# Attention into a sine-activated MLP on one core: alpha's load, the opening's casts and batch 1's transposes, x and v casts rearranged

## The chip, the cores and the metric

The kernel runs on one core of a Trainium2 chip, in one launch. The metric is the device time of an execution in microseconds (us). TensorE (PE) multiplies and transposes, VectorE (DVE), ScalarE (ACT) and GpSimd (POOL) do the rest, SyncE (SP) issues most of the DMAs, POOL some of them and ACT two.

## What is computed

```python
# q, k, v: (8 batches, 8 heads, 576 rows, 64); x: (4608, 512)
q_s = softmax(q, axis=-1)              # over the 64 entries of a head's row
k_s = softmax(k, axis=2)               # over the 576 rows
kv = einsum('bhsd,bhse->bhde', k_s, v) # a 64x64 matrix for each head
x = einsum('bhsd,bhde->bhse', q_s, kv) # transposed to (B*S, H*D) = (4608, 512)
h = x @ w_in                           # w_in (512, 2048)
g = h + sin(alpha * h)**2 / alpha      # alpha: 2048 values
out = g @ w_out                        # w_out (2048, 512), out (4608, 512)
```

The inputs are float32, the matmuls run in bf16.

## The kernel before, in words

The 4608 tokens are worked in nine stages t of 512 tokens. In a stage `mm_h` makes 16 tiles h (ni = 0 to 15), each by four 128x512 matmuls over the four column groups of x; ScalarE takes the sine (`sine`, L269), one of ScalarE, POOL and VectorE squares it (L271, L273, L275), VectorE combines it with h into g (`combine`, L279), and `mm_o` (L283) multiplies g by w_out, 64 matmuls to a stage. x comes from the attention of one batch at a time: exp of q and k on ScalarE (L119), v cast to bf16 with a column of ones, `kv_mm` (L174, 36 small matmuls for each half of the heads), `kv_norm` (L184, L185) which divides by the sums and gives `kbd`, q normalized (`qn`) and transposed (`tp`, L201, copied to `qT`), and `attn_x` (L218), whose result is copied to `xT`.

The order of the work on each engine is the order in which the program writes it. Nothing reorders it, so an instruction that waits holds up all that stand behind it on its engine. A DMA queue issues in that order too. PSUM banks come from pools of one or two buffers each ("a", "b", "l", "k"): a tile waits until the one before it in its buffer has been read.

**The opening** (L308 to L407) does batch 0. SyncE loads q, k and v in halves ("half" means the head pairs `ii` = 0 and 1), POOL the second half of v in two pieces (L308 from L341 and L342), then w_in in column pieces and w_out (L109, L112). ScalarE's queue loads alpha (L313), and TensorE transposes it ahead of everything else (L329); VectorE copies it and takes its reciprocal (L330, L331). The first x is copied to `xT` by VectorE and ScalarE (L393, L394), the second by VectorE twice (L405); ScalarE copies the second half of the transposed queries (L395) and casts the last four row blocks of v's second half, then loads the Sin table (L396). Of the tiles h, the parts that need only the first x run before the second x.

**Stage 0's tiles** (L407 to L460) carry the loads of batch 1 in `late`: after tile 6 the first half of q, after tile 8 and 10 pieces of w_out, after tile 13 the second half of q, and k and v in halves. A 1-element copy on VectorE into the tile (L443) makes the q loads wait for that place in VectorE's order, and SyncE's order makes the others wait behind them.

**Batch 1's attention** stands inside the 64 output matmuls of stage 0 (`o_quad`; `take(os, n)` puts the next n of them into TensorE's order). Here `norm_q` (L153) has POOL multiply the first half of q and VectorE the second; `cast_v1` (L474) casts one half of v on ScalarE and one on VectorE, all nine row blocks at a time; `transpose_q1` (L482) transposes one half and copies it on VectorE; `x_half` (L491) computes one half of x. After the first `kv_norm`, SyncE loads the leftover rows of q of batches 0 and 1 (`q8`, L497, again behind 1-element copies on VectorE, L496), and batch 2. After the second x, ScalarE takes exp of q8 and loads the Sin table again for stage 1 (L509). In stage 1, after tile 11, q8 is transposed (L523).

Of the kernel before, what the change touches and what calls it, by code (L numbers as in the profile page):

```python
# [15 lines left out]
F32 = mybir.dt.float32  # L16
BF16 = mybir.dt.bfloat16
# [6 lines left out]
def kernel(  # L24
# [78 lines left out]
        load("k", k, b)  # L103
        load("v", v, b)

    def load_win(c0, c1, k0=0, k1=4):
        n, kk = slice(c0, c1), slice(k0, k1)
        for x in range(2):
            nc.gpsimd.dma_start(out=win[64 * x:64 * x + 64, kk, n], in_=win_v[x][:, kk, n])  # L109

    def load_wout(n0, n1):
        nc.gpsimd.dma_start(out=wout[:, n0:n1, :], in_=wout_v[:, n0:n1, :])  # L112
# [66 lines left out]
    def kv_norm(b, i0=0, i1=2):  # L179

        kt, m = kbd[b % 2], i1 - i0
        kvr = small.tile([128, 2, 2], F32, name="kvr")[:, :, 0:m]
        src = A["kvp", b][:, :, i0 * 65:i1 * 65].rearrange("p e (ii c) -> p e ii c", ii=m)
        nc.vector.reciprocal(kvr, src[:, :, :, D])  # L184
        nc.vector.tensor_tensor(kt[:, :, i0:i1], src[:, :, :, 0:D],  # L185
                                kvr.unsqueeze(3).to_broadcast([128, 2, m, D]), op=ALU.mult)

    def q_tile(b):
        if ("qT", b) not in A:
            A["qT", b] = att2.tile([128, 2, J, 128], BF16, name="qT")  # L190
        return A["qT", b]
# [6 lines left out]
    def q_transpose_ii(b, ii, j0, j1, tp):  # L198

        for j in range(j0, j1):  # L200
            nc.tensor.transpose(tp[:, j - j0], A["qn", b][:, ii, j], identb)  # L201
# [108 lines left out]

    for n, t, ii in (("q", q, 0), ("k", k, 0), ("q", q, 1), ("v", v, 0), ("k", k, 1)):
        load0(nc.sync, n, t, ii, 0, 8 if n == "q" else J)
    nc.scalar.dma_start(out=alpha_rows, in_=moe_alpha.rearrange("(no ni) -> no ni", ni=128))  # L313
    make_identity(nc, ident)
    DVE_CP(identb, ident)
    zero = singles.tile([128, 1], F32, name="zero")
# [8 lines left out]

    tp0 = ps_h[0].tile([128, 8, 128], BF16, name="tp", tag="a")
    warm = ps_h[0].tile([128, 4, 128], F32, name="warm", tag="a")
    tpa = warm[:, 0, 0:nN]
    nc.tensor.transpose(tpa, alpha_rows, ident[0:nN, 0:nN])  # L329
    DVE_CP(alpha_sb, tpa)  # L330
    nc.vector.reciprocal(inva_sb, alpha_sb)  # L331

    def cast_v0(ii, j0, j1, eng):
        vv = vb[0].rearrange("p j (i c) -> p i j c", i=4)
        eng(vv[:, 2 * ii:2 * ii + 2, j0:j1, 0:D], staged["v", 0][:, ii::2, j0:j1])
# [2 lines left out]
    GP_CP(held, staged["k", 0][:, 0, 0, 0:1])  # L340
    load0(GP, "v", v, 1, 0, 5)  # L341
    load0(GP, "v", v, 1, 5, 9)  # L342
    for c0, c1 in ((0, 256), (256, 512), (512, 768), (768, 1024), (1024, 1536), (1536, 2048)):
        load_win(c0, c1)
    for c in range(2):
        load_wout(4 * c, 4 * c + 4)

    def warm_up(n):

        for _ in range(n):  # L350
            nc.tensor.matmul(warm, identb, A["qe", 0][:, 0:4, 0:128], start=True, stop=True)
# [30 lines left out]
    warm_up(2)  # L382
    kv_mm(0, 0, ps_k, split=True)
    warm_up(1)
    kv_norm(0, 0, 1)
    tp1 = ps_l.tile([128, 8, 128], BF16, name="tp", tag="l")
    q_transpose_ii(0, 1, 0, 8, tp1)
    cast_v0(1, 0, 5, DVE_CP)
    cast_v0(1, 5, 9, ACT_CP)

    xp = [bank("b") for _ in range(2)]
    attn_x(0, 0, 0, 8, xp)
    DVE_CP(xT[:, 0, 0:MF], xp[0])  # L393
    ACT_CP(xT[:, 2, 0:MF], xp[1])  # L394
    ACT_CP(A["qT", 0][:, 1, 0:8], tp1)  # L395
    nc.scalar.activation(zero, zero, AX.Sin)  # L396
    kv_mm(0, 1, ps_k, split=True)
    kv_norm(0, 1, 2)
    for ki in range(2):
        for ni in range(2):  # L400
            mm_h(0, ni, ki, ki + 1)
    xp = [bank("l") for _ in range(2)]
    attn_x(0, 1, 0, 8, xp)
    for x in range(2):
        DVE_CP(xT[:, 2 * x + 1, 0:MF], xp[x])  # L405
    for ki in range(2):
        for ni in range(2, 4):  # L407
            mm_h(0, ni, ki, ki + 1)

    def h_slot(t, ni, sq, lag):  # L410
        hp = mm_h(t, ni, 2 if ni < (4, 1, 0)[min(t, 2)] else 0)
# [18 lines left out]
    def take(it, n=1000):  # L430
        for _ in range(n):
            if next(it, 0) == 0:
                return
# [4 lines left out]
    with ES:  # L438
        def load_q1(ii):
            if ii == 0:  # L440
                staged["q", 1] = stage.tile([128, 4, J, D], F32, name="st_q", tag="st")
            st = staged["q", 1]
            DVE_CP(st[:, ii, 0, 0:1], zero)  # L443
            nc.sync.dma_start(out=st[:, ii::2, 0:8].rearrange("p i j d -> p i (j d)"),
                              in_=src_view(q, 1)[:, ii::2, 0:8 * D])

        def load_kv1():
            for n in "kv":
                staged[n, 1] = stage.tile([128, 4, J, D], F32, name=f"st_{n}", tag="st")
            for ii in range(2):  # L450
                for n, t in (("k", k), ("v", v)):
                    nc.sync.dma_start(out=staged[n, 1][:, ii::2].rearrange("p i j d -> p i (j d)"),
                                      in_=src_view(t, 1)[:, ii::2])

        late = {6: lambda: load_q1(0), 8: lambda: load_wout(8, 12), 10: lambda: load_wout(12, 14), 13: lambda: (load_q1(1), load_kv1())}
        for ni in range(nN):
            h_slot(0, ni, "DPPAPPAPPAAPPAPD"[ni], lag)
            flush(lag, 1)
            if ni in late:
                late[ni]()  # L460
        flush(lag, 0)

        accs = [bank(kind) for kind in "bbll"]
        os = o_quad(0, accs, [DVE_CP, ACT_CP, DVE_CP, DVE_CP])
        take(os, 46)
        for ii in range(2):
            exp_half("q", 1, ii, 8)
        norm_q(1, [GP, V], 8)
        GP_CP(held, staged["k", 1][:, 0, 0, 0:1])
        load_wout(14, 16)  # L470

        def cast_v1(ii, eng):
            vv = vb[1].rearrange("p j (i c) -> p i j c", i=4)
            eng(vv[:, 2 * ii:2 * ii + 2, :, 0:D], staged["v", 1][:, ii::2])  # L474

        exp_half("k", 1, 0)
        cast_v1(0, ACT_CP)
        exp_half("k", 1, 1)
        def transpose_q1(ii):
            tp = ps_h[0].tile([128, 8, 128], BF16, name="tp", tag="a")  # L480
            q_transpose_ii(1, ii, 0, 8, tp)
            DVE_CP(q_tile(1)[:, ii, 0:8], tp)  # L482

        transpose_q1(0)
        take(os, 4)

        def x_half(ii):
            xp = [bank("a") for _ in range(2)]
            attn_x(1, ii, 0, 8, xp)
            for x in range(2):  # L490
                (ACT_CP, DVE_CP)[x](xT[:, 2 * x + ii, MF:2 * MF], xp[x])  # L491

        kv_mm(1, 0, ps_k, split=True)
        kv_norm(1, 0, 1)
        for b in range(2):
            DVE_CP(q8[:, 0, b, 0:1], zero)  # L496
            nc.sync.dma_start(out=q8[:, :, b], in_=src_view(q, b)[:, :, 8 * D:J * D])  # L497
        load_batch(2)
        cast_v1(1, DVE_CP)
        take(os, 4)  # L500
        x_half(0)
        take(os, 2)
        transpose_q1(1)
        kv_mm(1, 1, ps_k, split=True)
        kv_norm(1, 1, 2)
        take(os, 5)
        x_half(1)
        exp_to(A["qe", 1][:, J - 2:J], q8)
        nc.scalar.activation(zero, zero, AX.Sin)  # L509
        take(os)  # L510
        for ki in range(2):
            mm_h(1, 0, ki, ki + 1)
        norm_q8()
        load("q", q, 3)
        load("k", k, 3)
        load("v", v, 3)

        def late_q8(ni):
            if ni == 11:
                tp = ps_k.tile([128, 2, 2, 128], BF16, name="tp", tag="a")  # L520
                for b in range(2):
                    for ii in range(2):
                        nc.tensor.transpose(tp[:, ii, b], A["qe", 1][:, J - 2 + b, ii * 128:(ii + 1) * 128], identb)  # L523
                DVE_CP(A["qT", 1][:, :, J - 2:J], tp)
            elif ni == 15:
                xp = ps_k.tile([128, 2, 512], F32, name="xp", tag="a")
                for ii in range(2):
                    for b in range(2):
                        for e in range(2):
                            for x in range(2):  # L530
                                r, c = slice(64 * x, 64 * x + 64), (2 * ii + b) * P
                                nc.tensor.matmul(xp[64 * e:64 * e + 64, x, c:c + P], kbd[b][r, e, ii],
                                                 A["qT", 1][r, ii, J - 2 + b, e * 64:(e + 1) * 64],
                                                 start=True, stop=True)
                DVE_CP(xT[:, :, 16 * P:18 * P].rearrange("p (x i) n -> p x i n", x=2),
                       xp[:, :, 0:4 * P].rearrange("p x (i n) -> p x i n", i=2))

        for ni in range(nN):
            h_slot(1, ni, SQ[ni], lag)
            flush(lag, 1)  # L540
            late_q8(ni)
        cast_v(2, [GP_CP, GP_CP])
        flush(lag, 0)
# [149 lines left out]
```

## Time and profile before

| | us |
|---|---|
| median of 3 runs (lowest, highest) | 282.85 (282.79, 283.14) |
| the profiled execution | 283.53 |
| its span, first to last instruction | 281.7 |
| TensorE busy in it (1890 matmuls) | 268.6 |
| ScalarE, VectorE, POOL busy | 224.1, 185.4, 83.5 |
| stage 0's output matmuls start | 28.00 |
| batch 1's first kv matmul | 40.25 |
| stage 1's first matmul | 45.85 |
| stage 1's first sine | 47.93 |

Stage 1 means t = 1. All times within a run are counted from the first instruction. A line of a timeline has the start, the length, the engine, the line of the kernel, the operation, what it writes and reads, how many instructions were merged, and in brackets how long the engine sat idle before it and what ended that. A DMA's landing is the moment at which its completion was signalled. Successive 128x512 matmuls start 0.216 us apart, though each is shown with a length of 0.38, since they are pipelined; some matmul records are missing.

### The profile page before, as it was taken

Reading aid. Unit: us, or ns where it says so; the run is one execution under the profiler, and the core shown is the slowest. Engines: PE = TensorE matmul, PEld = TensorE weight load, DVE = VectorE, ACT = ScalarE, POOL = GpSimd, SP = SyncE. Lnnn points to the kernel's source line nnn. Section 1 sums busy time; section 2 is a strip of 40 time slices with the busy share of each in tenths; the row PEclk is TensorE's granted clock in tenths of the full one; section 3 lists DMA queues with packets and bytes.
Section 4 is the critical chain, followed back from the end, with each engine's and each line's share of the span. In section 5 each row is a group of like instructions: output and inputs, shape, how many; then the busy total and the mean of one; then the engine's idle time right before and its main releaser. Section 6 shows DMA issues by size and latency. Waiting matters only on the chain.

```text
span 281.7 us, 4930 instructions
## 1 busy us (share of the span) xinstructions
PE 268.6 (95%) x1890; PEld 124.2 (44%) x1919; DVE 185.4 (66%) x280; ACT 224.1 (80%) x320; POOL 83.5 (30%) x80
## 2 busy tenths in 40 slices
PE   2999989999999999999999999999999999999994
PEld 1444444444444444444544444444444444444443
DVE  3868658799868767766866677567675555555412
ACT  4989466999588999899989998999877777777400
POOL 1989410777666550115003500341000000000000
PEclk9999999999999999999999999999999999999999
DMA  7999989996699129811991199125011111111143
GB/s 260 308 187 230 296 288 310 360 329 252 142 171 396 62 61 326 316 37 40 277 381 43 37 249 403 32 57 123 1 36 40 37 37 37 40 38 42 41 106 74
DMA packets 39128, 45.82 MB, mean 163 GB/s; under 512 B 17072, under 2 KB 22464, under 8 KB 39104
## 3 DMA queue, kind: packets, MB, share of 16 engines
q1 hardware_dynamic: 33360, 40.57, 46.6%
q0 software_dynamic: 5552, 4.79, 10.2%
q8 instruction: 15, 0.25, 0.3%
q10 hardware_dynamic: 192, 0.14, 0.2%
q14 instruction: 9, 0.07, 0.1%
HBM read 36.71 MB, written 9.44 MB: 164 GB/s over the span
## 4 chain that ended last, share of the span: by engine, by line
PE 85%; DMA 5%; DVE 4%; ACT 2%; issue 2%; POOL 1%; SPq 0%; ACTq 0%
PE op L283 38%; PE hp L263 37%; DMA st_v<-in_v_dram 3%; PE kvp L174 2%; PE lp L263 2%; DMA st_q<-in_q_dram 1%; POOL s L273 1%; PE op L263 1%; PE op L663 1%; ACT s L269 1%; PE hp L218 1%; PE kvp L263 1%; DVE qs L364 1%; DVE qn L366 1%; PE xp L218 1%
## 5 line engine op out<-in xcount | busy, mean ns | idle before, releaser
L279 DVE SCALAR_TENSOR_TENSOR g<-s,inva_sb,hp 128x512 bf16<-128x512 f32 x128 | 94.5, 745 | 58.8 <-ACT s L271 53.3
L263 PE MATMUL hp<-xT,win 128*128 128x512 bf16 x505 | 127.4, 379 | 0.7 <-DVE kvr L184 0.3
L283 PE MATMUL op<-wout,g 128*128 128x512 bf16 x478 | 121.0, 379 | 1.6 <-issue 1.1
L269 ACT ACTIVATE s<-hp,alpha_sb 128x512 f32<-128x512 f32 x128 | 86.2, 682 | 23.3 <-PE hp L263 21.9
L263 PEld LDWEIGHTS <-win 128*128 128x128 bf16 x576 | 55.9, 98 | 68.0 <-issue 1.7
L283 PEld LDWEIGHTS <-g 128*128 128x128 bf16 x560 | 53.2, 98 | 64.7 <-issue 2.3
L271 ACT ACTIVATE s<-s 128x512 f32<-128x512 f32 x112 | 70.5, 630 | 3.6
L273 POOL TENSOR_TENSOR s<-s 128x512 f32<-128x512 f32 x29 | 30.1, 1056 | 21.8 <-ACT s L269 21.8
L153 POOL TENSOR_TENSOR qn<-qe,qs 128x1152 bf16<-128x1152 bf16 (+1 forms) x12 | 25.1, 2111 | 34.0 <-DVE qs L147 25.3
L295 DVE COPY o<-op 128x512 f32<-128x512 f32 (+2 forms) x33 | 21.8, 660 | 10.2 <-PE op L283 7.9
L138 POOL CAST vb<-st_v 128x1152 bf16<-128x1152 f32 x12 | 14.7, 1259 | 44.7 <-DMA st_v<-in_v_dram 44.7
L119 ACT ACTIVATE qe<-st_q 128x1152 bf16<-128x1152 f32 (+2 forms) x18 | 17.7, 1024 | 6.2 <-DMA st_q<-in_q_dram 6.0
L119 ACT ACTIVATE ke<-st_k 128x1152 bf16<-128x1152 f32 x16 | 17.9, 1151 | 0.9 <-DMA st_k<-in_k_dram 0.9
L146 DVE TENSOR_REDUCE qs<-qe 128x36 f32<-128x2304 bf16 x5 | 12.8, 2551 | 8.3 <-ACT qe L119 8.3
L119 ACT ACT_TABLE_LOAD x7 | 9.0, 1283 | 1.3 <-PEq L677 1.2
L283 PE MATMUL hp<-wout,g 128*128 128x512 bf16 x31 | 8.8, 379 | 0.1
L283 PE MATMUL lp<-wout,g 128*128 128x512 bf16 x30 | 8.6, 380 | 0.2 <-issue 0.2
L174 PEld LDWEIGHTS <-ke 64*64 64x64 bf16 x576 | 5.8, 106 | 5.3 <-issue 2.1
L174 PE MATMUL kvp<-vb,ke 64*64 64x65 bf16 x576 | 6.9, 194 | 1.1 <-ACT vb L474 0.8
L263 PE MATMUL lp<-xT,win 128*128 128x512 bf16 x31 | 7.5, 379 | 0.1
L109 POOL DMA_DIRECT2D win<-in_moe_w_in_dram x12 | 7.4, 701 | 0.0
L231 DVE CAST xT<-xp 128x1024 bf16<-128x1024 f32 (+1 forms) x7 | 7.4, 1065 | 0.0
(86 smaller groups left out, 133.5 us busy)
## 6 DMA issues: line engine op xcount, KB each, us to landing
out_dram<-o SPq DMA_DIRECT2D x70, 128.0 KB, 2.4
st_q<-in_q_dram SPq DMA_DIRECT2D x6, 1152.0 KB, 6.2
st_k<-in_k_dram SPq DMA_DIRECT2D x6, 1152.0 KB, 8.6
st_v<-in_v_dram SPq DMA_DIRECT2D x6, 1152.0 KB, 11.1
st_k<-in_k_dram SPq DMA_DIRECT2D x4, 576.0 KB, 7.3
st_q<-in_q_dram SPq DMA_DIRECT2D x4, 512.0 KB, 5.9
st_v<-in_v_dram SPq DMA_DIRECT2D x3, 576.0 KB, 8.7
wout<-in_moe_w_out_dram POOLq DMA_DIRECT2D x3, 512.0 KB, 10.4
```

The lines of the kernel that those rows point to most:

```text
L119: nc.scalar.activation(dst[:, :, ii * 128:(ii + 1) * 128].rearrange("p j (x d) -> p x j d", x=2), src[:, ii::2], AX.Exp)
L138: engs[ii](vv[:, 2 * ii:2 * ii + 2, :, 0:D], staged["v", b][:, ii::2])
L146: nc.vector.tensor_reduce(qs, A["qe", b].rearrange("p j (i d) -> p j i d", i=4), axis=AXL.X, op=ALU.add)
L153: engs[ii % len(engs)].tensor_tensor(qn[:, ii, 0:j1].rearrange("p j (x d) -> p j x d", x=2), qe[:, ii], part.unsqueeze(3).to_broadcast([12 ...
L174: nc.tensor.matmul(kvp[64 * x:64 * x + 64, e, ii * 65:(ii + 1) * 65], ke[r, j, h * 64:(h + 1) * 64], vt[r, j, h * 65:(h + 1) * 65], start= ...
L263: nc.tensor.matmul(hp, win[:, KO[k], ni * 128:(ni + 1) * 128], xT[:, KO[k], t * MF % NX:t * MF % NX + MF], start=(k == 0), stop=(k == 3))
L269: nc.scalar.activation(s, hp, AX.Sin, scale=alpha_sb[:, ni:ni + 1])
L271: nc.scalar.activation(s, s, AX.Square)
L273: nc.gpsimd.tensor_tensor(s, s, s, op=ALU.mult)
L279: nc.vector.scalar_tensor_tensor(G[t][:, ni], in0=s, scalar=inva_sb[:, ni:ni + 1], in1=hp, op0=ALU.mult, op1=ALU.add)
L283: nc.tensor.matmul(acc, G[t][:, ni, j * 128:(j + 1) * 128], wout[:, ni, :], start=(ni == 0), stop=(ni == nN - 1))
L295: eng(o[:, cols], acc)
```

## The change

- alpha's load goes from ScalarE's queue to SyncE's, as the sixth DMA there. Its transpose goes behind the first `kv_mm` in TensorE's order, its copy to ScalarE, and its reciprocal behind the second `kv_norm` on VectorE.
- In the opening VectorE casts both pieces of v's second half and copies the second half of the transposed queries; ScalarE copies both parts of the first x and one of the two parts of the second. The Sin table is loaded after these. Three parts of tiles h instead of four stand before the second x.
- All loads of batch 1 are let go after tile 11, the first half of q among them.
- In batch 1, both halves of q are multiplied on VectorE, the second after the first `kv_norm`. ScalarE casts five row blocks of each half of v and POOL the other four. ScalarE copies the first half of the transposes. The first x follows the first kv after two output matmuls instead of four; the second transposes stay behind it, now two output matmuls ahead of the second kv instead of right ahead of it. q8's loads and batch 2's come after the first x.
- `load_win` loses two arguments that were not used; it issues the same DMAs.

```diff
-    nc.scalar.dma_start(out=alpha_rows, in_=moe_alpha.rearrange("(no ni) -> no ni", ni=128))
+    nc.sync.dma_start(out=alpha_rows, in_=moe_alpha.rearrange("(no ni) -> no ni", ni=128))
...
-    tpa = warm[:, 0, 0:nN]
-    nc.tensor.transpose(tpa, alpha_rows, ident[0:nN, 0:nN])
-    DVE_CP(alpha_sb, tpa)
-    nc.vector.reciprocal(inva_sb, alpha_sb)
...
     warm_up(1)
+    tpa = warm[:, 0, 0:nN]
+    nc.tensor.transpose(tpa, alpha_rows, ident[0:nN, 0:nN])
     kv_norm(0, 0, 1)
     tp1 = ps_l.tile([128, 8, 128], BF16, name="tp", tag="l")
     q_transpose_ii(0, 1, 0, 8, tp1)
+    ACT_CP(alpha_sb, tpa)
     cast_v0(1, 0, 5, DVE_CP)
-    cast_v0(1, 5, 9, ACT_CP)
+    cast_v0(1, 5, 9, DVE_CP)
+    DVE_CP(A["qT", 0][:, 1, 0:8], tp1)

     xp = [bank("b") for _ in range(2)]
     attn_x(0, 0, 0, 8, xp)
-    DVE_CP(xT[:, 0, 0:MF], xp[0])
-    ACT_CP(xT[:, 2, 0:MF], xp[1])
-    ACT_CP(A["qT", 0][:, 1, 0:8], tp1)
-    nc.scalar.activation(zero, zero, AX.Sin)
+    for x in range(2):
+        ACT_CP(xT[:, 2 * x, 0:MF], xp[x])
     kv_mm(0, 1, ps_k, split=True)
     kv_norm(0, 1, 2)
-    for ki in range(2):
-        for ni in range(2):
-            mm_h(0, ni, ki, ki + 1)
+    nc.vector.reciprocal(inva_sb, alpha_sb)
+    for ni, ki in ((0, 0), (1, 0), (0, 1)):
+        mm_h(0, ni, ki, ki + 1)
     xp = [bank("l") for _ in range(2)]
     attn_x(0, 1, 0, 8, xp)
     for x in range(2):
-        DVE_CP(xT[:, 2 * x + 1, 0:MF], xp[x])
-    for ki in range(2):
-        for ni in range(2, 4):
-            mm_h(0, ni, ki, ki + 1)
+        (ACT_CP, DVE_CP)[x](xT[:, 2 * x + 1, 0:MF], xp[x])
+    nc.scalar.activation(zero, zero, AX.Sin)
+    for ni, ki in ((1, 1), (2, 0), (2, 1), (3, 0), (3, 1)):
+        mm_h(0, ni, ki, ki + 1)
...
-        late = {6: lambda: load_q1(0), 8: lambda: load_wout(8, 12), 10: lambda: load_wout(12, 14), 13: lambda: (load_q1(1), load_kv1())}
+        late = {8: lambda: load_wout(8, 12), 10: lambda: load_wout(12, 14), 11: lambda: (load_q1(0), load_q1(1), load_kv1())}
...
-        take(os, 46)
-        for ii in range(2):
-            exp_half("q", 1, ii, 8)
-        norm_q(1, [GP, V], 8)
-        GP_CP(held, staged["k", 1][:, 0, 0, 0:1])
-        load_wout(14, 16)
-        exp_half("k", 1, 0)
-        cast_v1(0, ACT_CP)
-        exp_half("k", 1, 1)
-        transpose_q1(0)
-        take(os, 4)
-        kv_mm(1, 0, ps_k, split=True)
-        kv_norm(1, 0, 1)
-        (q8's loads, load_batch(2))
-        cast_v1(1, DVE_CP)
-        take(os, 4)
-        x_half(0)
-        take(os, 2)
-        transpose_q1(1)
-        kv_mm(1, 1, ps_k, split=True)
-        kv_norm(1, 1, 2)
-        take(os, 5)
-        x_half(1)
+        def cast_v1(ii):
+            vv = vb[1].rearrange("p j (i c) -> p i j c", i=4)
+            for j0, j1, eng in ((0, 5, ACT_CP), (5, 9, GP_CP)):
+                eng(vv[:, 2 * ii:2 * ii + 2, j0:j1, 0:D], staged["v", 1][:, ii::2, j0:j1])
...
+        def q1_sums(ii):
+            part, src = qs1[:, :, 2 * ii:2 * ii + 2], qe1[:, ii]
+            nc.vector.tensor_reduce(part, src, axis=AXL.X, op=ALU.add)
+            nc.vector.reciprocal(part, part)
+
+        def q1_norm(ii):
+            part = qs1[:, :, 2 * ii:2 * ii + 2]
+            nc.vector.tensor_tensor(A["qn", 1][:, ii, 0:8].rearrange("p j (x d) -> p j x d", x=2), qe1[:, ii],
+                                    part.unsqueeze(3).to_broadcast([128, 8, 2, D]), op=ALU.mult)
+
+        take(os, 44)
+        for ii in range(2):
+            exp_half("q", 1, ii, 8)
...
+        GP_CP(held, staged["k", 1][:, 0, 0, 0:1])
+        load_wout(14, 16)
+        q1_sums(0)
+        q1_norm(0)
+        q1_sums(1)
+        exp_half("k", 1, 0)
+        cast_v1(0)
+        transpose_q1(0, ACT_CP)
+        exp_half("k", 1, 1)
+        take(os, 4)
+        kv_mm(1, 0, ps_k, split=True)
+        kv_norm(1, 0, 1)
+        q1_norm(1)
+        take(os, 2)
+        x_half(0)
+        cast_v1(1)
+        (q8's loads, load_batch(2))
+        take(os, 4)
+        transpose_q1(1, DVE_CP)
+        take(os, 2)
+        kv_mm(1, 1, ps_k, split=True)
+        kv_norm(1, 1, 2)
+        take(os, 4)
+        x_half(1)
```

The last part of the diff is written out by order of the program, without the lines that only moved between functions; "(q8's loads, load_batch(2))" stands for four lines that are the same on both sides.

More of the change, by code (lines that the diff above doesn't have):

```diff
@@ L104, in load_batch, with load_win @@
         load("v", v, b)
-    def load_win(c0, c1, k0=0, k1=4):
-        n, kk = slice(c0, c1), slice(k0, k1)
+    def load_win(c0, c1):
         for x in range(2):
-            nc.gpsimd.dma_start(out=win[64 * x:64 * x + 64, kk, n], in_=win_v[x][:, kk, n])
+            nc.gpsimd.dma_start(out=win[64 * x:64 * x + 64, :, c0:c1], in_=win_v[x][:, :, c0:c1])
     def load_wout(n0, n1):
@@ L342 @@
     load0(GP, "v", v, 1, 5, 9)
-    for c0, c1 in ((0, 256), (256, 512), (512, 768), (768, 1024), (1024, 1536), (1536, 2048)):
-        load_win(c0, c1)
+    for c in range(4):
+        load_win(256 * c, 256 * c + 256)
+    for c in range(2, 4):
+        load_win(512 * c, 512 * c + 512)
     for c in range(2):
@@ L464, with transpose_q1 @@
         os = o_quad(0, accs, [DVE_CP, ACT_CP, DVE_CP, DVE_CP])
-        take(os, 46)
-        for ii in range(2):
-            exp_half("q", 1, ii, 8)
-        norm_q(1, [GP, V], 8)
-        GP_CP(held, staged["k", 1][:, 0, 0, 0:1])
-        load_wout(14, 16)
-        def cast_v1(ii, eng):
-            vv = vb[1].rearrange("p j (i c) -> p i j c", i=4)
-            eng(vv[:, 2 * ii:2 * ii + 2, :, 0:D], staged["v", 1][:, ii::2])
-        exp_half("k", 1, 0)
-        cast_v1(0, ACT_CP)
-        exp_half("k", 1, 1)
-        def transpose_q1(ii):
+        def cast_v1(ii):
+            vv = vb[1].rearrange("p j (i c) -> p i j c", i=4)
+            for j0, j1, eng in ((0, 5, ACT_CP), (5, 9, GP_CP)):
+                eng(vv[:, 2 * ii:2 * ii + 2, j0:j1, 0:D], staged["v", 1][:, ii::2, j0:j1])
+        def transpose_q1(ii, eng):
             tp = ps_h[0].tile([128, 8, 128], BF16, name="tp", tag="a")
             q_transpose_ii(1, ii, 0, 8, tp)
-            DVE_CP(q_tile(1)[:, ii, 0:8], tp)
-        transpose_q1(0)
-        take(os, 4)
+            eng(q_tile(1)[:, ii, 0:8], tp)
         def x_half(ii):
@@ L491, in x_half @@
                 (ACT_CP, DVE_CP)[x](xT[:, 2 * x + ii, MF:2 * MF], xp[x])
+        def q1_sums(ii):
[9 more added lines that the diff above has]
+            exp_half("q", 1, ii, 8)
+        qe1 = A["qe", 1][:, 0:8].rearrange("p j (ii x d) -> p ii j x d", ii=2, x=2)
+        A["qn", 1] = att1.tile([128, 2, J, 2 * D], BF16, name="qn")
+        qs1 = small.tile([128, 8, 4], F32, name="qs1")
+        GP_CP(held, staged["k", 1][:, 0, 0, 0:1])
[8 more added lines that the diff above has]
+        take(os, 4)
         kv_mm(1, 0, ps_k, split=True)
         kv_norm(1, 0, 1)
+        q1_norm(1)
+        take(os, 2)
+        x_half(0)
+        cast_v1(1)
         for b in range(2):
```

## The prediction, made before the changed kernel was run

> **What bounds the kernel now.** I read the page first, then the chain of waits from 15 to 57 us, then the queues of the first 60 us, then the timelines of single engines.
>
> ```profile
> span 281.7 us, 4930 instructions
> ...
> PE   2999989999999999999999999999999999999994
> ...
> PE 85%; DMA 5%; DVE 4%; ACT 2%; issue 2%; POOL 1%; SPq 0%; ACTq 0%
> ```
>
> TensorE carries 85% of the chain. In the trace its 128x512 matmuls follow each other every 0.216 us from 16.13 to 39.24 and, but for changes of tile form, from 45.85 to the end. So the time moves only where that stream is late: before 16.13, between 39.24 and 45.85 (batch 1's kv and x put into the stream), and at later stalls. The chain says what delays it:
>
> ```profile
> 28.53 0.75 DVE g L279
> 29.37 0.37 SPq L444
> 29.78 0.47 SPq L452
> 30.30 8.71 DMA st_v<-in_v_dram
> 39.03 1.18 ACT vb L474
> 40.25 0.48 PE kvp L174 x35
> ...
> 42.09 0.58 ACT xT L491
> 42.72 0.61 PE tp L201 x8
> ...
> 56.41 0.38 PE tp L523 x4
> ```
>
> (start, length, what). The trace has TensorE's last matmul before the kv starting at 39.02 and the kv at 40.25; such a change of form takes 0.31 elsewhere, so TensorE was ready at 39.33 and 0.92 is lost. It waits for ScalarE's cast of batch 1's first half of v, and that for the transfer. The queues of the first 60 us, in 40 slices of 1.5 us:
>
> ```profile
> DMA  0599999999999999999999999993689999999589
> GB/s 0 126 402 407 411 407 429 239 174 182 162 182 206 205 199 208 203 220 337 228 207 283 408 406 412 399 268 59 141 203 362 398 408 403 358 386 407 154 195 361
> ```
>
> From 3 to 40.5 us the DMA engines have no free slice. This decides most of what follows: what is loaded until v's first half must pass, in whatever order, and no earlier TensorE makes it pass sooner.
>
> **The opening** (alpha's load and transpose, shared casts). Gone from ScalarE: a DMA issue of 0.45 (hidden: it waits 2.4 for q next), a cast of v (0.61) and the queries' copy (1.02); added: two xT copies of 0.59 and a 128x16 copy (about 0.2, as the 128x1 row of 0.20). VectorE gets that cast (0.59 as 512/640 of its 0.74) and the queries' copy at its 0.69, and gives up two xT copies of 0.69 and alpha's small ones. Worked through: qT ready at 13.5 instead of 14.13, kbd at 14.0 instead of 13.65 (its reciprocal now stands behind that copy), second x at 14.13 instead of 14.34; its two copies then run side by side (14.58 to 15.27) instead of in series (14.79 to 16.08), so the stream is unbroken 0.27 earlier than 16.13. The Sin table (1.28) now loads after the copy, 15.1 to 16.4, and the first sine stays at 16.5. But the gain ends soon:
>
> ```profile
> 20.97 6.70 PEld L263 LDWEIGHTS <-win 128*128 128x128 bf16 x32 [0.21 <-issue]
> ```
>
> These are the weights of tile 8. Their transfer landed at 20.87 by the trace, the load follows 0.1 later, the matmul at 21.10. TensorE meets that transfer 0.27 earlier and waits. The full queue lands v's first half when it did, and the 0.92 would take the rest. Value: 0; bounds 0 and -0.27. The cost side is covered too: alpha, sixth on SyncE's queue, lands not before k's second half (10.50) and, at worst, after v's last piece (11.95). Its transpose stands before eight others in TensorE's queue, with the first x and the second kv behind them, so these come up to 0.9 late (11.95 against 11.03). The same 0.92 covers that; what goes beyond counts in full.
>
> **Loads of batch 1.** The first q load moves from 23.20 to after tile 10's combine; that ends at 26.96, so all six issue from 27.05 to 29.4 (before: q at 23.20 and 29.37, the rest to 31.3). The engines are full either way, and the same bytes stand before v's first half, so k, v, k, v land at 36.6, 39.0, 40.4, 42.0 as now. q's first half is later: the second landed at 35.2 and 512 KB take 1.3 us at 400 GB/s, so 33.8; bounds 32.9 (27.05 plus the 5.8 of the second half) and 35.2. Then exp 1.06, sum 1.22, reciprocal 0.25, product 1.22 on VectorE (instead of 1.91 on POOL): 37.8. The transposes are needed at 37.5 (two matmuls fewer stand before them), and with 0.44 for them, four matmuls and the change of form TensorE is ready for kv at 39.2, before v is cast. Nothing is lost until q lands after 34.4.
>
> **Batch 1, from v's landing (39.01), before -> after:**
> - Cast: 1.17 on ScalarE -> five of nine blocks there, 0.72 by interpolation between 0.61 (128x512) and 1.17 (128x1152); POOL's four: 0.52 as its share of 1.17, at most 1.02 as the share of 2.29, its row beside a VectorE product at 68.59. I take 0.6; it runs beside ScalarE's. kv matmuls at 40.25 -> 39.80.
> - kbd ready 41.29 -> 40.84. ScalarE copies the transposes after its cast, 1.02, to 40.70. Two matmuls, then first x: 41.63 -> 40.97.
> - ScalarE: exp of k's second half 1.16 to 41.75, xT copy to 42.2. That frees the bank: second transposes 42.72 -> 42.26. In between four matmuls to 42.17.
> - ScalarE's part of v's second cast (landed 42.0) now follows the xT copy: done 42.85 (VectorE: 42.79 before). The kv matmuls, after two more of the output, 43.26 -> 43.23: nearly all is given back, since TensorE again changes form between transposes and kv (0.31 instead of 0.15).
> - Four matmuls instead of five, second x 44.85 -> 44.60; four left instead of three (+0.22): the next stage's first matmul 45.85 -> 45.80. Sum: -0.05.
>
> The Trainium skill, "GPSIMD Engine Reference", Specifications, says POOL shares its SBUF interfaces with VectorE where VectorE reads two SBUF inputs. The row above agrees (2.29 instead of 1.17, and VectorE's product 1.97 beside it); it would bite if a product met a cast, and on my schedule none does (40.8 to 42.0 against 42.0).
>
> **The next stage's sines.** On VectorE the two marks that let q8's loads go now stand behind the second product (1.22) and an xT copy (0.68): 41.20 -> 42.7, so q8's second load issues at 43.3 instead of 41.84. It landed 3.0 after issue, behind leftovers of v and wout; the first took 2.3. Hence 45.6 to 46.3. ScalarE is free for its exp at 45.7, before 45.79; from there table and first sine are fixed (2.15 later). Shift of the sines: -0.1 to +0.5; I take +0.15, nearer the first row since the queue is empty by then. This reaches TensorE: its transposes at 56.41 (L523) need the bank that VectorE's combine of tile 7 frees at 55.62 + 0.74 = 56.36, and that hangs on POOL's squares, back to back at 1.04, and so on the first sines. TensorE itself was ready at 56.2. So +0.15 there, and then to the end. The 1.5 us by which the loads of batches 2 and 3 slip behind q8 on SyncE's queue are covered: batch 2's q landed at 48.5 and is read at 62.75; batch 3's v, read at 68.59 by a POOL that is free until 74.1, is the tightest.
>
> **Sum.** Opening 0, loads 0, batch 1 -0.05 (hidden by the next), sines +0.15: 283.53 (span 281.7 and 1.8 around it) becomes 283.7 for the profiled run. That run lies 0.7 above the median of 282.85; on the median: **283.0**. A measurement of this kernel can tell about 0.2% (0.57 us) from no change.
>
> **Rivals.**
> 1. *v lands earlier.* The six loads are queued 1.9 us sooner, while about 1.3 us of POOL's wout transfers still stand before them; if these give way beyond v's landing, v comes up to 1 us earlier. For: q's first load, issued at 23.20, had its packets from 26.5 on, in the midst of wout's. Against: all of wout was served before q's second load, and sharing leaves the same bytes ahead. TensorE can use at most 0.9 (with q earlier too it is ready at 38.9 instead of 39.8): 282.1.
> 2. *q8 becomes the bound* (slower): two loads of 256-byte rows late behind VectorE's product. With 3.56, the longest of the 128 KB stores nearby (64.81), it lands at 46.9, sines +1.0, TensorE at 56.41 +1.0: up to 283.9, typically 283.6. It decides from a landing after 46.3.
> 3. *q's first half becomes the bound* (slower): landing at 35.2 instead of 33.8 makes the transposes 39.2 and kv 40.6: +0.8, 283.8.
> 4. *The opening counts*: if tile 8's weights and v both come earlier, -0.3: 282.6.
>
> **How the numbers follow.** Forecast 283.0 (282.5 to 283.4): 0.47, rival 4 included. Rival 1: 0.27. Rivals 2 and 3: 0.17 and 0.09. So faster 0.27, same 0.47, slower 0.26. The range 282.0 to 283.9 takes in rivals 1 to 3 to their usual ends.
>
> **What would show it.** Right: no hole in the matmuls before kv; kv's matmuls about 0.8 after v's landing near 39.0; tile 8's weights still met at 20.97; the first sine of the next stage within 0.5 of 47.93. Wrong: a v landing away from 39.0 by over 0.5, q landing after 34.4, POOL's cast above 1 us, or a hole before the transposes at 56.41 over 0.5.

## The result, and the profile after

The changed kernel takes 284.37 us (median of 13 runs, 283.05 to 285.22), the kernel before 282.81 on the same chip (13 runs, 282.50 to 283.59): a ratio of 1.0054, interval 1.0043 to 1.0064. By the medians it is slower by 1.6 us. The forecast of 283.0 was wrong, and the time lies above its range, which ended at 283.9.

The page of the changed kernel's profile (an execution of 284.73):

```profile
span 282.9 us, 4934 instructions
PE   2899989989999999999999999999999999999994
PE 80%; DMA 7%; POOL 5%; issue 4%; DVE 2%; SPq 0%; ACT 0%; POOLq 0%
```

TensorE's share of the chain has gone from 85% to 80%. Its chain of waits from 15 to 60 us (start, length, what):

```profile
27.09 0.33 SPq L443
...
28.12 9.38 DMA st_k<-in_k_dram
37.50 0.05 issue
37.55 1.10 POOL held L497
38.65 0.70 POOL wout L111
39.35 0.63 POOL vb L468
...
42.73 7.24 issue
...
54.88 2.73 DVE g L278 x4
...
57.66 0.38 PE tp L539 x4
```

The chain goes through q8's transposes (L539; L523 before), as in the kernel before. Here it reaches them over VectorE's combines and POOL's squares, which hang on the sines. Further back it is to be read with care: the 7.24 of "issue" is POOL idle until ScalarE's first sine, which this view does not follow. TensorE's own timeline shows where it stood still:

```profile
38.66 0.62 PE L200 MATMUL tp<-identb,qn 128*128 128x128 bf16 x8 [1.06 <-DVE qn L488]
...
40.08 0.48 PE L173 MATMUL kvp<-vb,ke 64*64 64x65 bf16 x36
...
57.66 0.38 PE L539 MATMUL tp<-identb,qe 128*128 128x128 bf16 x4 [0.95 <-DVE g L278]
```

There are two new holes of about 1 us, one at batch 1's first transposes and one at q8's. ScalarE's timeline leads from each to a landing:

```profile
34.75 1.06 ACT L118 ACTIVATE qe<-st_q 128x1024 bf16<-128x1024 f32 x1 [4.11 <-DMA st_q<-in_q_dram]
...
45.33 0.59 ACT L479 CAST xT<-hp 128x512 bf16<-128x512 f32 x1
47.11 0.72 ACT L118 ACTIVATE qe<-q 128x256 bf16<-128x256 f32 x2 [1.20 <-DVE o L294]
47.85 1.28 ACT L525 ACT_TABLE_LOAD   x1
49.15 0.20 ACT L525 ACTIVATE zero<-zero 128x1 f32<-128x1 f32 x1
49.26 0.67 ACT L268 ACTIVATE s<-kvp,alpha_sb 128x512 f32<-128x512 f32 x1
```

q's first half landed at 34.73. q8's exp waited until 47.11. The releaser named there is a copy of VectorE's that ended at the same moment, but the exp reads nothing of it: q8's second load landed at 47.01, and in all nine other profiles in which ScalarE waits here (eight of the runs below and a second one of this kernel) the exp starts 0.10 to 0.11 after that landing. ScalarE had nothing to do from 45.9.

### The profile page after: what moved, and what is told of

It reads as the page before. It is cut to its first block, busy times and chain, and to the rows that moved or that the text cites. A ratio compares the mean times of both kernels' runs of the same rounds, so it can differ in the third digit from the quotient of the medians.

```text
span 282.9 us, 4934 instructions
## 1 busy us (share of the span) xinstructions
PE 268.0 (95%) x1890; PEld 123.6 (44%) x1919; DVE 184.8 (65%) x278; ACT 224.7 (79%) x323; POOL 83.9 (30%) x81
## 3 DMA queue, kind: packets, MB, share of 16 engines
q0 software_dynamic: 5552, 4.79, 10.4%
HBM read 36.71 MB, written 9.44 MB: 163 GB/s over the span
## 4 chain that ended last, share of the span: by engine, by line
PE 80%; DMA 7%; POOL 5%; issue 4%; DVE 2%; SPq 0%; ACT 0%; POOLq 0%
PE op L282 38%; PE hp L262 36%; DMA st_k<-in_k_dram 5%; POOL s L272 2%; DMA win<-in_moe_w_in_dram 2%; DVE g L278 2%; PE kvp L173 2%; PE op L262 1%; PE op L679 1%; PE hp L217 1%; POOL win L108 1%; PE xp L217 1%; PE lp L262 1%; POOL st_v L307 1%; POOL vb L468 1%
## 5 line engine op out<-in xcount | busy, mean ns | idle before, releaser
L152 POOL TENSOR_TENSOR qn<-qe,qs 128x1152 bf16<-128x1152 bf16 x11 | 23.2, 2128 | 29.6 <-DVE qs L146 24.5
L294 DVE COPY o<-op 128x512 f32<-128x512 f32 (+2 forms) x33 | 21.8, 661 | 10.2 <-PE op L282 7.9
L348 PE MATMUL warm<-qe,identb 128*128 128x512 bf16 x10 | 4.1, 552 | 5.2 <-ACT qe L118 5.2
```

What stands on the lines that cost most here:

```text
L152: engs[ii % len(engs)].tensor_tensor(qn[:, ii, 0:j1].rearrange("p j (x d) -> p j x d", x=2), qe[:, ii], part.unsqueeze(3).to_broadcast([12 ...
L294: eng(o[:, cols], acc)
```

## The experiments

The expectations speak of theory A (q8's loads, now behind the first x, hold up stage 1's sines), theory B (q's first half, now behind tile 11, lands too late) and C (both). Each comparison is with the kernel before on the same chip. "Early" and "late" mean the places of the kernel before and of the change.

**Undoing one part, or doing one part alone.** First q8's place undone in the changed kernel:

```diff
         kv_norm(1, 0, 1)
+        (q8's marks and loads, load_batch(2))
         q1_norm(1)
         take(os, 2)
         x_half(0)
         cast_v1(1)
-        (q8's marks and loads, load_batch(2))
```

> The changed kernel with one thing undone: the marks and loads of q8, and batch 2's loads behind them, stand right behind the first kv_norm again, ahead of the second product on VectorE. Theory A (q8's late landing delays stage 1's sines, and these TensorE at the transposes of q8): the loads issue near 41.1 and 41.6 instead of 42.9 and 43.4, land by 45.2, the first sine starts at 47.9 to 48.1 instead of 49.26, and the time falls by 1.1 to 1.4 to 283.0 to 283.3. Theory B (the hole of 1.1 us ahead of batch 1's first transposes, from the late first half of q, is what costs): that hole stays, so the time stays at 284.2 to 284.5.

Measured: 283.64, ratio 1.0020 (0.9996 to 1.0045). q8's wait is gone from the profile; the hole at the first transposes stays (1.3). About 0.7 us came back by the medians, 1.0 by the ratios: the time lies between the two forecasts, so neither theory alone holds.

Then the same move made in the kernel before, from behind `kv_norm(1, 0, 1)` to behind `x_half(0)`:

```diff
         kv_norm(1, 0, 1)
-        (q8's marks and loads, load_batch(2))
         cast_v1(1, DVE_CP)
         take(os, 4)
         x_half(0)
+        (q8's marks and loads, load_batch(2))
```

> The kernel before with only q8's marks and loads (and batch 2's) moved behind the first x and its copies. Theory A: the marks wait for VectorE's xT copy, end near 43.4, the second load lands near 47, the first sine moves from 47.93 to 49.1 to 49.7, and the time rises by 1.0 to 1.7 to 283.8 to 284.5. Theory B: q's first half is loaded as before, nothing before the transposes changes, so 282.8 (282.6 to 283.0).

Measured: 283.89, 1.0034 (1.0010 to 1.0058). The one wait in its batch 1 and stage 1 is 0.9 at q8's transposes. Theory B alone falls.

The list of late loads as before, in the changed kernel:

```diff
-late = {8: .., 10: .., 11: lambda: (load_q1(0), load_q1(1), load_kv1())}
+late = {6: lambda: load_q1(0), 8: .., 10: .., 13: lambda: (load_q1(1), load_kv1())}
```

> The changed kernel with batch 1's loads let go as before: q's first half after tile 6, the rest after tile 13. Theory A: the hole ahead of the first transposes goes, but v lands when it did and q8's loads stay late, so the first sine stays within 0.3 of 49.26 and the time at 284.0 to 284.5. Theory B: the time falls by 0.8 to 1.1 to 283.3 to 283.6.

Measured: 283.07, 1.0013 (0.9995 to 1.0032). No wait at the transposes. Theory A alone falls. In the profile, of an execution at 282.56, q8's second load landed at 44.85, just ahead of stage 1's first matmul at 44.92, and the first sine came at 47.10: this execution paid next to nothing for q8's later place.

The reverse, that list of the change in the kernel before:

> The kernel before, with the changed kernel's list of late loads alone (q's first half behind tile 11 of stage 0, in one row with the second half, k and v). Theory C: q's first half lands near 34.7, batch 1's first transposes wait for it behind the last product of the o matmuls, 0.7 to 1.2 us; q8's marks move back with it, but q8's place in the order is the early one: 283.4 to 284.0. Rival, only q8's place costs (theory A): 282.8, within 0.2 of the kernel before. Rival, the sharing of work in the opening and the copies costs too: this kernel has none of it, so it comes out lower than the changed kernel with q8 early (283.64) by what that sharing costs.

Measured: 285.42, 1.0093 (1.0075 to 1.0111), worse than the whole change and above every forecast. TensorE's timeline, then POOL's:

```profile
40.24 0.62 PE L201 MATMUL tp<-identb,qn 128*128 128x128 bf16 x8 [1.77 <-POOL qn L153]
```

```profile
38.27 1.91 POOL L153 TENSOR_TENSOR qn<-qe,qs 128x1024 bf16<-128x1024 bf16 x1 [8.01 <-DVE qs L152]
40.13 1.19 POOL L469 COPY held<-st_k 128x1 f32<-128x1 f32 x1
```

q's first half landed at 35.48, and here the product that follows is POOL's 1.91. So the new order of batch 1, with VectorE's product of 1.22, makes late q cheaper; that gain shows only where q is late.

Both moves undone in the changed kernel:

> The changed kernel with both moves undone: q's first half is issued as early as in the kernel before (as in the run that undid this alone, 283.07), and q8's marks and loads and batch 2's loads stand right behind the first normalisation of kv (as in the run that undid that alone, 283.64). Theory C, late q and late q8 in series, one path: the two undoings are not worth their sum. With q early, ScalarE is free of its x copies at 44.9 and both pieces of q8 have landed by then (44.34, 44.85), so an earlier q8 brings the first sine nothing: 282.9 to 283.2. Rival, two independent losses: 0.7 and 1.3 us add up, 284.37 - 2.0 = 282.3 to 282.5.

Measured: 282.67, 0.9988 (0.9968 to 1.0009). The four kernels with the change's order and the three with the old one make a table of ratios:

| | q early, q8 early | q early, q8 late | q late, q8 early | both late |
|---|---|---|---|---|
| batch 1 as before | 1 | 1.0034 | 1.0093 | not run |
| batch 1 as changed | 0.9988 | 1.0013 | 1.0020 | 1.0054 |

In the last row late q8 costs 0.0025 and 0.0034 (0.7 and 1.0 us), late q 0.0032 and 0.0041 (0.9 and 1.2). Of these differences 0.0034 and 0.0041 are clear of zero, 0.0025 and 0.0032 lie within the intervals of their two runs. Undone one at a time, the moves are worth 0.0034 and 0.0041, together 0.0075; undone both, 0.0066. So the prices add up within the intervals, but the measured 282.67 lies between the forecast of theory C and that of two independent losses, and does not settle between them. What is left of the change without the two moves does not differ measurably from the kernel before.

The opening alone, in the kernel before:

> The kernel before with the change's opening alone: alpha on SyncE's queue and its transpose behind the first kv, the opening's casts and copies shared anew, the order of stage 0's first chunks; batch 1 and the list of late loads as before. The prediction's step: worth nothing, since tile 8's w_in columns and v's landing absorb what the opening gains: 282.8, within 0.2. Rival (the prediction's fourth): the opening counts, up to 0.27 less: 282.5 to 282.6. Rival: the new sharing delays the first x by a copy that no profile of this core showed: 283.0 or more.

Measured: 282.80 against 282.93, 0.9994 (0.9979 to 1.0010). It is worth nothing that can be measured; the interval leaves room for the 0.27 of the prediction's fourth rival.

**What late q is.** Only q's first half moved back, to tile 6 (23.1, the edit shown), and then only to tile 9:

```diff
-late = {8: .., 10: .., 11: lambda: (load_q1(0), load_q1(1), load_kv1())}
+late = {6: lambda: load_q1(0), 8: .., 10: .., 11: lambda: (load_q1(1), load_kv1())}
```

> The changed kernel with q's first half alone issued early (behind tile 6 of stage 0, as in the kernel before); its second half, k and v stay behind tile 11. Theory: of the loads put together, q's first half is the one that TensorE waits for. It lands near 29.8, the transposes need no wait, q8 follows: 282.9 to 283.3, as with all the gating undone (283.07). Rival, it is the early start of k, v and the second half that is harmful (contention with the w_out loads, landings 34 to 42): 284.0 to 284.4.

> The changed kernel with q's first half alone issued earlier, behind tile 9 of stage 0 (near 25.3) instead of behind tile 11 (27.04); behind tile 6 (23.1) it landed at 29.73 and gave 283.33. If what counts is only that it lands ahead of some 33.9 (the last product of the o matmuls less the chain of exp, sum, reciprocal and product), then 25.3 and 7.2 us make 32.5, and the time is as with tile 6: 283.1 to 283.5. If what counts is that its packets go ahead of w_out's pieces of tiles 8 and 10, it lands later than 33.9 and the time is near the changed kernel's: 284.0 or more.

Measured: tile 6 gives 283.33, 1.0015 (1.0004 to 1.0027); tile 9 284.56, 1.0055 (1.0036 to 1.0075), no better than tile 11. Behind tile 9 it issued at 26.02, landed at 34.11 after 8.09, and v landed at 39.12; behind tile 6 it landed at 29.73 and v at 37.88. My guess of 25.3 plus 7.2 failed: the load took longer, and its first packet ran at 28.88, against 26.61 behind tile 6. So issuing q a little earlier is not enough; as behind tile 11, the engines read little between 27 and 33 (step 2 below). Behind tile 9 TensorE waits 0.2 for q and 0.4 for v; that profile is of the fastest of its eight executions, at 283.75, so it does not show where the others lost more.

To separate q from v, q's first half early and the rest behind tile 14:

> The changed kernel with q's first half early (behind tile 6 of stage 0) and its second half, k and v a good deal later (behind tile 14, one tile later than in the kernel before), so that v lands near 39, as in the changed kernel, but TensorE finds its first transposes' operand ready. If late q costs by TensorE's wait for q itself: 283.1 to 283.4, as in the two runs with q early (283.07, 283.33). If it costs as much by v, which lands after q's first half on the same queue: 283.9 to 284.5.

Measured: 283.75 against 283.37 on that chip, 1.0019 (0.9989 to 1.0049). The interval holds both answers, so the split between q's and v's lateness stays open. Its profile, of an execution at 284.15, shows that v's part can exist (v landed at 38.82), but q8's transposes waited 0.86 in it too, so its time is not v's alone:

```profile
39.62 0.48 PE L173 MATMUL kvp<-vb,ke 64*64 64x65 bf16 x36 [0.65 <-ACT vb L468]
```

**Second looks at the two kernels, unchanged.**

> The kernel before, unchanged, in a second profiled execution. The prediction's arithmetic took from the first one that v of batch 1 lands at 39.01, 1.2 us after TensorE could have used it, so that nothing ahead of it counts. With the opening changed alone the same loads of the same batch 1 landed at 36.04, 37.44, 39.28 and 40.65. If the first profile showed a rare landing: v near 37.5 to 38.1, no wait of kv for it over 0.5, time 282.4 to 283.0. If it is the usual one: v at 38.7 to 39.2 and the wait of about 1.2 again.

> The changed kernel, unchanged, in a second profiled execution: whether q's first half lands past 34.4 again (first profile 34.73), with TensorE's hole of about 1.2 us at batch 1's first transposes, and whether q8's second load takes 3.6 us again. If both are the kernel's own: hole 0.9 to 1.5, and a landing of q8 past 45.7. If q8's 3.61 us was one execution's scatter: 2.6 to 3.1 here, and TensorE's wait at q8's transposes under 0.5.

Measured: before 282.78. v landed at 37.64 and TensorE waited for nothing; its timeline, against the 40.25 of the first profile:

```profile
38.16 0.61 PE L201 MATMUL tp<-identb,qn 128*128 128x128 bf16 x8
38.61 0.59 PE L283 MATMUL lp<-wout,g 128*128 128x512 bf16 x2
39.04 0.59 PE L283 MATMUL hp<-wout,g 128*128 128x512 bf16 x2
39.56 0.48 PE L174 MATMUL kvp<-vb,ke 64*64 64x65 bf16 x36
```

The changed kernel 284.97. q landed at 35.30, and q8's second load took 2.60 instead of 3.61 (landed 46.58):

```profile
39.24 0.62 PE L200 MATMUL tp<-identb,qn 128*128 128x128 bf16 x8 [1.71 <-DVE qn L488]
...
57.24 0.39 PE L539 MATMUL tp<-identb,qe 128*128 128x128 bf16 x4 [0.18 <-DVE g L278]
```

So the hole at q is the kernel's own, 1.1 to 1.7; q8's varies, 0.95 in the first profile and 0.18 here. From batch 2 on, this execution lost 0.5 more at a first x that waited for the transposing DMA of batch 2's queries.

**Three tries to get around q8.** Batch 2's loads behind the second x, so that q8's have the queues to themselves:

> The changed kernel with batch 2's loads moved from right behind q8's loads to behind the second x; q8's own place is unchanged. This asks why q8's second load took 3.6 us from issue to landing. If batch 2's loads, queued right behind it, hold up its last rows: it lands 2.3 to 3.0 after its issue at 43.4, so 45.7 to 46.4, the first sine starts at 47.9 to 48.6 and the time is 283.0 to 283.7. If the load is slow by itself: it lands at 47.0, and the time stays at 284.2 to 284.5.

Measured: 284.85, 1.0066 (1.0040 to 1.0091). The time lies above both forecasts. q8's second load took 2.64 and TensorE's wait for it fell to 0.2, but the unmoved loads gave 2.60 and 0.2 in the second profile above, so this does not show that batch 2's loads slow it. And batch 2's q came too late for its own x. TensorE's waits from 56 to 80 us (what, for whom, total, times, longest):

```profile
PE hp L217 <- DVE qs L145: 0.8, 1, 0.8
PE tp L539 <- DVE g L278: 0.2, 1, 0.2
```

q8's transposes one tile later (`if ni == 12` for `if ni == 11`):

> The changed kernel with q8's four transposes on TensorE behind tile 12 of stage 1 instead of behind tile 11. They take the bank of tile 7, and wait for its combine. If late q8 is paid at this one place, because a bank is asked for out of the tiles' order, tile 12's 0.86 us of matmuls now stand ahead of the wait, and 0.8 of the 1.0 us waited there go: 283.4 to 283.8. If ScalarE's lag behind TensorE is a lasting one, the wait shows up at a later tile or at stage 1's end: 284.2 to 284.5.

Measured: 284.40, 1.0059 (1.0036 to 1.0082). Nothing gained. In the profile, of the fastest of its nine executions, q8's second load landed at 45.77, 0.06 after stage 1's first matmul, so there was little wait to save at the transposes. A new one came behind them, at the small x of q8, which needs VectorE's copy of those transposes:

```profile
PE xp L548 <- DVE qT L540: 0.5, 1, 0.5
```

Everything early, and q8's exp ahead of the second x's copies:

> The changed kernel with q early, q8's two loads behind the first normalisation of kv (batch 2's loads stay where the change put them), and q8's exponential ahead of the second x's copies on ScalarE instead of behind them. If the first sine is bound by ScalarE's chain (x copy, two exps of 0.42, table 1.28), 0.7 us of that chain go ahead into ScalarE's idle time from 42 to 43.8, the first sine comes 0.6 to 0.7 sooner behind stage 1's start (1.5 instead of 2.2), TensorE's gap of 0.45 at q8's transposes closes to 0.22 or so: 282.5 to 282.9. If q8's second piece lands after 44.3, the exp holds the x copy up, and it is 283.0 or more. If the sines have no part in it: as with q and q8 early, 283.1.

Measured: 282.67, 0.9997 (0.9987 to 1.0008). The first sine did not come sooner (47.09, 2.00 after stage 1's start): ScalarE stood idle until 43.99 for the output's copy (L294) ahead of the exp, so the exp went into no idle time. No version beats the kernel before by more than its interval.

## Why the prediction was wrong, step by step

Two terms of its sum failed. "Loads 0" cost 0.9 or 1.2 us by the ratios above; in the changed kernel's two profiles TensorE waits 1.06 and 1.71 for q's first half. "Sines +0.15" cost 0.7 or 1.0. The first was set against a slack that the kernel before does not usually have. Two of its own signs of being wrong came: q landed after 34.4, and the hole at q8's transposes was over 0.5.

1. **The baseline.** "The full queue lands v's first half when it did, and the 0.92 would take the rest." The 0.92 belonged to that one execution. In the second profile, and with the opening alone (v at 37.44), there is no wait for v; in the seven profiles with the old list of loads v landed at 37.44 to 39.01, and the prediction's is the latest. The prediction took the slack from the slow execution and then subtracted 0.7 "on the median", though the wait for v was itself what made that execution slow. What was to be hidden behind v had no cover.

2. **"The engines are full either way, and the same bytes stand before v's first half."** This is the step under "loads 0" that failed. For 27 to 30 and 30 to 33 us (window, length, busy time and count of PE, PEld, DVE, ACT and POOL, clock, DMA share, GB/s), the kernel before in its second profile, then the changed one:

```profile
27.00:30.00 3.00, 3.00 (x16) 1.34 (x15) 2.17 (x5) 2.95 (x6) 2.65 (x3) 1.00 1.15 285
30.00:33.00 3.00, 3.00 (x16) 1.34 (x15) 3.00 (x5) 1.93 (x2) 0.12 (x1) 1.00 1.21 246
```

```profile
27.00:30.00 3.00, 3.00 (x16) 1.37 (x14) 2.30 (x6) 2.95 (x5) 2.53 (x3) 1.00 1.15 176
30.00:33.00 3.00, 3.00 (x16) 1.36 (x14) 1.85 (x3) 0.64 (x1) 0.00 (x0) 1.00 1.09 268
```

The DMA share from 27 to 30 is the same 1.15, the bytes are 285 against 176 GB/s. By queue (packets, MB, share) in the two windows, before (second profile) and after; q0 carries w_out here, q1 the loads of q, k and v:

```profile
q0 software_dynamic: 358, 0.35, 70.2%
q1 hardware_dynamic: 261, 0.50, 44.9%
...
q0 software_dynamic: 517, 0.50, 100.7%
q1 hardware_dynamic: 117, 0.24, 20.7%
```

```profile
q0 software_dynamic: 534, 0.53, 115.2%
...
q0 software_dynamic: 286, 0.27, 61.3%
q1 hardware_dynamic: 270, 0.53, 48.1%
```

These bytes are to be read with care. w_in and w_out are float32 and become bf16 in their loads, and the view counts those at two bytes a number, as two rows of the page of the changed kernel show:

```profile
q0 software_dynamic: 5552, 4.79, 10.4%
HBM read 36.71 MB, written 9.44 MB: 163 GB/s over the span
```

4.79 MB are w_in and w_out at two bytes (4.19) and the 0.59 of v's second half in the opening; 36.71 MB are all inputs at four. So a slice at about 205 GB/s with w_out alone is no idle half: 410 are read in it. With w_out at four bytes, the kernel before reads 400 GB/s (2 x 0.35 and 0.50 MB in 3 us) and 413 in the two windows, as from 33 to 36 (410), and the changed one 353 and 357, at a share of 1.15 and 1.09. Busy is not throughput.

Before, q's first half (issued at 23.43) has its packets here from 26.57 on. After, q issued at 27.04 and its first packet ran at 30.68; until then w_out's ran alone, and slower than before 27. Why they slow down there is open. In the nine profiles with q's first half issued near 23 the engines read 2.39 to 2.46 MB from 27 to 33 (w_out at four bytes again), in the seven with it behind tile 9 or 11 2.03 to 2.19. The 0.31 MB that are missing by 33 in the two profiles shown are 0.8 us at 400 GB/s, and v landed at 38.89 and 41.81 (second profile 39.50 and 42.32) instead of 37.64 and 41.29. That v's first half landed near the forecast 39.0 is luck: the forecast was a late landing of the kernel before, left unchanged, and the change made a usual one late. The Trainium skill, "Perfetto Trace Analysis", Identifying the Most-Contended Engine, says to go by HBM utilization for DMA, since occupancy misleads with 16 engines; these windows agree, with 400 and 353 GB/s at one share.

3. **"512 KB take 1.3 us at 400 GB/s, so 33.8"** for q's first half. It landed at 34.73 and 35.30. The chain behind it took what was worked out (landing to transposes 3.93, forecast 4.0). "Nothing is lost until q lands after 34.4" counted on the cover of step 1; the transposes stood still as soon as their operand came after 37.5. Rival 3 had the mechanism, and for a landing at 35.2 its times too (transposes 39.2, kv 40.6; the second profile has 35.30, 39.24 and 40.65). Its price of 0.8 was counted from a kv that waits for v; the holes were 1.06 and 1.71.

4. **"Shift of the sines: -0.1 to +0.5; I take +0.15."** Against stage 1's start it was +1.2 in the first profile and +0.2 in the second. q8's second load issued at 43.40 and 43.98 (forecast 43.3; in the second profile all of batch 1 stood later, by the hole at q) and took 3.61 and 2.60 (forecast 3.0, or the 2.3 of the first). In the first profile the issue was near the forecast, and the mis-sized term is the time to the landing; rival 2 had 3.56 for it and a shift of 1.0. In us, by profiled execution:

| | landing of q8 less stage 1's first matmul | first sine less the same | wait at q8's transposes |
|---|---|---|---|
| before, second profile | -0.79 | 2.08 | none |
| both undone | -1.31 | 2.01 | none |
| changed, second profile | 0.05 | 2.30 | 0.18 |
| kernel before, q8 late | 0.74 | 3.03 | 0.9 |
| changed | 1.06 | 3.31 | 0.95 |

In these rows a landing 0.8 or more ahead of stage 1 costs nothing, one at its start 0.2, and from there on every 0.1 us shifts the sines by about 0.1.

5. **The rivals** 2 and 3 were priced as alternatives (0.17 and 0.09). In the first profile they came together, and in the ratios their prices add up within the intervals. Against the second profile of before, the changed kernel's last matmul is 1.95 later: -0.29 up to the output matmuls of stage 0, +1.07 from there to stage 1's first matmul, +1.17 after it. For its own second profile these are -0.36, +1.72 and +0.84.

6. **What held**: the casts of v's first half (0.74 and 0.63 for a forecast of 0.72 and 0.6), and the opening at 0, this one not for the reasons given. Tile 8's weights were met again in the changed kernel, with a longer idle time of the weight loads before them:

```profile
21.01 0.99 PEld L262 LDWEIGHTS <-win 128*128 128x128 bf16 x6 [0.57 <-issue]
```

But with the opening alone (its profile is of the fastest of twelve executions) neither these weights nor v held TensorE up, and stage 0's output matmuls started at 27.59. They start at 27.59 to 28.31, on average 27.9, in the twelve profiles with the new opening, and at 28.00 to 28.40, on average 28.25, in the four with the old one. So some 0.3 us may be gained there, which the times of whole executions do not resolve.

Open is why q8's second load needs between 2.6 and 3.7 us, and 4.4 with q late in the kernel before. That its scatter explains the runs above 283.9 with q early and q8 late (3 of 12) is only argued: the profile is of an execution at 282.56.

## What to carry to other kernels

Take slack from more than one execution: a wait that makes the profiled run slower than the median is not cover for anything. Where DMA engines are busy throughout, compare the bytes of a window before and after, and first ask at which size a load that casts is counted: a slice at half the rate may be a full one. When a change moves two loads back, price the case in which both come late, not each alone.

## What the runs showed of the hardware

POOL's 1-element copy that holds back w_out's last load takes 0.19 us where VectorE is not in a product, and 1.10 beside one (the kernel before in its second profile, then the changed one, with its second cast of v):

```profile
36.29 0.19 POOL L469 COPY held<-st_k 128x1 f32<-128x1 f32 x1 [0.65 <-DMA st_k<-in_k_dram]
```

```profile
37.55 1.10 POOL L497 COPY held<-st_k 128x1 f32<-128x1 f32 x1 [7.67 <-DMA st_k<-in_k_dram]
...
41.87 0.86 POOL L468 CAST vb<-st_v 128x512 bf16<-128x512 f32 x1 [1.89 <-DMA st_v<-in_v_dram]
```

VectorE's product of two bf16 operands ran from 37.38 to 38.60 there, and the copy ended at 38.65. In the six other profiles where they met, the copy ended 0.04 to 0.05 after the product too: it took 1.10 to 1.19 in five, and 0.30 in one where it began 0.25 before the product's end. The prediction had said that no product meets a cast. POOL's second cast did meet one (41.03 to 42.25) and took 0.86 instead of 0.63, and the copy ahead of the first cast, at which the prediction had not looked, lost more. The Trainium skill, "GPSIMD Engine Reference", Specifications, tells of the shared interface that the prediction had cited; these rows show that it holds up even one element a partition until the product ends.

A load of q's first half on SyncE's queue had its first packet 2.9 to 3.8 us after its issue in all 16 profiles (23.43 to 26.57, 27.04 to 30.68), while w_out's packets kept the engines busy.
